# First-pass iteration of an attention backward kernel: order of the matrix products, transposes and scores on TensorE, and the e column on GpSimd

## The chip, the cores and the metric

The kernel runs on one core of a Trainium2 chip. The metric is device microseconds of one execution. Before the change the median of four runs is 932.12 us (931.36 to 933.66).

## The reference

One decode step (one query position, B = 2, H = 32 heads, 4096 cached positions, head size 128) of a block with layer norm, attention and a small MLP, and the gradients of all its inputs. What costs time is the cache: K and V have 64 pairs (b, h) of 1 MB each, and their gradients are of the same size.

```python
scores = jnp.einsum("bhqd,bhkd->bhqk", q, k) * (Dh ** -0.5)
p = _softmax(scores, axis=-1)
o = jnp.einsum("bhqk,bhkd->bhqd", p, v)
...
h = x + _A_ref(_layernorm(x, axis=-1), A_k_cache, A_v_cache, A_wq, A_wo)
h2 = h + _B_ref(_layernorm(h, axis=-1), B_w1, B_w2)
...
_out, _vjp = jax.vjp(_f, A_x, A_k_cache, A_v_cache, A_wq, A_wo, B_w1, B_w2)
```

## The kernel before, in words

**Two passes.** The first pass goes over the 64 pairs once. For a pair it reads K and V (1 MB each, laid out as 128 partitions x 32 chunks x 128), computes scores, softmax numerators, the attention output, and two things that the backward pass needs later: a 128x128 matrix m = V^T (e K) with one more column for V^T e, and u = e^T K. The second pass goes over the pairs again, reads V (`Wt`; the last 6 and 5 heads of the two batches are kept in SBUF instead), and writes the gradients gK and gV, 1 MB each. It starts while the first pass is still running: from first-pass iteration 41 (`P2_AT = H + 2 + 7`) on, every second iteration carries one second-pass pair ("mixed" stage), and after the first pass the second runs alone.

**An iteration of the first pass** (`p1_iter`, lines 463 to 587) is software-pipelined over three pairs. For the newest pair (`c`, pair i) it makes scores; for the pair before (`p`, pair i-1) it makes the exponentials e and the product e K; for the pair before that (`r`, pair i-2) it makes m and u. This document uses short names for the groups of TensorE work:

- T0 to T3: `transpose_group`, eight 128x128 transposes of K chunks into a PSUM bank (L416). Two banks take turns. Each group is then copied to SBUF (`t_sb`, called KT0 to KT3 here) by ScalarE (L421), or the fourth by VectorE (L419) while i < 33.
- S0 to S3: `matvec_group`, eight matmuls with one column that make 8 x 128 scores from KT0 to KT3 (L427).
- M0 to M7: `m_part`, four matmuls with 129 columns each (L471).
- u: `u_part`, eight matmuls (L496).
- mx: one matmul that spreads the row maxima (L513). It needs `rmax` of pair i-1, a VectorE reduction (L562) over the scores after S3.

After mx come, one after the other, `nb` (VectorE, L515), the exponential `ep` (ScalarE, L521), and two products `pk` = e K of half a pair each (`pk_half(0)` and `pk_half(1)`, VectorE, L478). Into the 129th column of each `pk` half goes e itself (the "e column", `pk_tile`, L486). A copy of e for the second pass goes to `P_bf` (L567; on GpSimd while i < 41, then on VectorE).

**What sets the order.** The schedule is manual: each engine runs its instructions in the order in which the program emits them. `p1_iter` is a generator with eight steps, k = 0 to 7. After each step the main loop (L1185 to L1202) calls `pump` (which emits the next loads on the SP queue, as far as buffers have been given back), emits background work (`bg_step`: layer norm, MLP, the L650 reductions on VectorE, called ttr here), and in the mixed stage one or two steps of the second-pass generator `p2_iter` (after steps 1, 3, 4 and 6). On TensorE the order before is

T0 T1 | mx M0 | S0 T2 M1 | S1 M2 T3 | u M3 S2 M4 | M5 S3 | M6 | M7

with a bar where a step ends. On VectorE it is nb, pk_half(0), KT3 copy (while i < 33), rmax, pk_half(1).

**Buffers.** Twelve 1 MB SBUF buffers serve K, V and W loads. A K buffer is given back after `pk_half(1)` of the next iteration (L571), a V buffer after M7 two iterations later (L581), and kept V tiles are not given back until the second pass has used them. The `pk` halves take turns in three buffers, so `pk_half(1)` and its e column must wait until M3 and u have read the half that was in that buffer.

Of the kernel before, what the change touches and what calls it, by code (L numbers as in the profile page):

```python
# [15 lines left out]
def kernel(  # L16
# [20 lines left out]
    nc = tc.nc  # L37
# [15 lines left out]
    HALF = NSC // 2  # L53
    GH = 8
    OG = 4
# [17 lines left out]
    def pst(shape, dtype, role, name):  # L73

        k = banks[role].pop(0)
        banks[role].append(k)
        return ps.tile(shape, dtype, tag=f"bank{k}", bufs=1, name=name)
# [19 lines left out]
    def goes_to(tag):  # L97

        if owned[tag] > wanted.get(tag, len(pools)):
            for other in homes:  # L100
                if owned[other] < wanted.get(other, 0):
                    return other
        return tag

    def give(t, to=None):
        tag, k, _ = home_of.pop(id(t))
        to = to or goes_to(tag)
        owned[tag] -= 1
        owned[to] += 1
        free[to] += 1  # L110
        homes[to].append(k)
        given_at[k] = step[0]
# [92 lines left out]
    rt = cols.tile([128, B, H], FP32)  # L205
# [3 lines left out]
    P_bf = cols.tile([128, B * H, NSC], BF16)  # L209
# [194 lines left out]
    def warm(dst, nat, g, busy):  # L404


        for k in range(busy):
            nc.tensor.matmul(dst, lhsT=nat[:, g * GT, :],
                             rhs=nat[:, g * GT + 4 * k:g * GT + 4 * k + 4, :].rearrange("p a b -> p (a b)"),
                             start=True, stop=True)  # L410

    def transpose_group(nat, g, dve=False, busy=0):
        t_ps = pst([128, GT, 128], BF16, "tps", "t_ps")
        warm(t_ps[:].bitcast(FP32).rearrange("p a b -> p (a b)"), nat, g, busy)
        for j in range(GT):
            nc.tensor.transpose(t_ps[:, j, :], nat[:, g * GT + j, :], ident_bf[:])  # L416
        t_sb = mats.tile([128, GT, 128], BF16, tag="XT", bufs=5, name="t_sb")
        if dve:
            nc.vector.tensor_copy(out=t_sb[:], in_=t_ps[:])  # L419
        else:  # L420
            nc.scalar.copy(out=t_sb[:], in_=t_ps[:])  # L421
        return t_sb

    def matvec_group(dst, t_sb, g, vec):
        for j in range(GT):
            sc = g * GT + j
            nc.tensor.matmul(dst[:, sc:sc + 1], lhsT=t_sb[:, j, :], rhs=vec, start=True, stop=True)  # L427
# [35 lines left out]
    def p1_iter(i, dve_group, busy):  # L463

        c = S1[i] if i < NP1 else None
        p = S1[i - 1] if 1 <= i <= NP1 else None
        r = S1[i - 2] if i >= 2 else None

        def m_part(k):
            for sc in range(4 * k, 4 * k + 4):  # L470
                nc.tensor.matmul(r["m"][:, 0:129], lhsT=r["V"][:, sc, :],  # L471
                                 rhs=r["pk"][sc // HALF][:, sc % HALF, 0:129],
                                 start=(sc == 0), stop=(sc == NSC - 1))

        def pk_half(k):

            sl = slice(k * HALF, (k + 1) * HALF)
            nc.vector.tensor_tensor(  # L478
                out=p["pk"][k][:, :, 0:128].rearrange("p s (a two) -> p s a two", two=2),
                in0=p["K"][:, sl, :].rearrange("p s (a two) -> p s a two", two=2),  # L480
                in1=p["ep"][:, sl, None, :].to_broadcast([128, HALF, 64, 2]), op=ALU.mult)

        def pk_tile(k):

            pk = pkp.tile([128, HALF, 130], BF16, tag="pK", bufs=3, name="pk")
            nc.scalar.copy(out=pk[:, :, 128:129], in_=p["ep"][:, k * HALF:(k + 1) * HALF, 0:1])  # L486
            p["pk"].append(pk)

        def u_part():

            br, hr = pairs[i - 2]
            if hr == 0:
                u_bank[0] = pst([128, 512], FP32, "u", "u_ps")
            for k in range(8):
                g = k % 4
                nc.tensor.matmul(u_bank[0][32 * g:32 * g + H, :], lhsT=hot[:, H - 1 - hr:2 * H - 1 - hr],  # L496
                                 rhs=r["pk"][k // 4][:, 4 * g:4 * g + 4, 0:128],
                                 start=(hr == 0 and k < 4), stop=(hr == H - 1 and k >= 4))

        if c is not None:  # L500
            b, h = pairs[i]
            q = qc[:, h, b:b + 1]
            c["KT0"] = transpose_group(c["K"], 0, busy=busy)
            c["KT1"] = transpose_group(c["K"], 1)
        yield
        if r is not None:
            r["m"] = pst([128, 132], FP32, "m", "m_ps")
        if p is not None:

            bp, hp = pairs[i - 1]  # L510
            bhp = bp * H + hp
            mx = p["bank"][:, 64:192]
            nc.tensor.matmul(mx, lhsT=p["rmax"][:].to_broadcast([128, 128]), rhs=neg_ident[:], start=True, stop=True)  # L513
            nb = small.tile([128, 1], FP32, tag="nb", name="nb")
            nc.vector.tensor_reduce(out=nb[:], in_=mx, axis=AX.X, op=ALU.min)  # L515
        if r is not None:
            m_part(0)
        yield
        if p is not None:
            ep = small.tile([128, NSC, 2], BF16, tag="ep", name="ep")  # L520
            nc.scalar.activation(out=ep[:], in_=p["s"][:, :, None].to_broadcast([128, NSC, 2]),  # L521
                                 func=ACT.Exp, bias=nb[:], scale=SCALE, accum_out=es[:, bp, hp:hp + 1])
            p["ep"] = ep
            p["pk"] = []
            pk_tile(0)
        if c is not None:
            c["bank"] = pst([128, 512], FP32, "sps", "s_ps")
            c["s"] = c["bank"][:, 0:NSC]
            matvec_group(c["s"], c.pop("KT0"), 0, q)
            c["KT2"] = transpose_group(c["K"], 2, busy=busy)  # L530
        if r is not None:
            m_part(1)
        yield
        if c is not None:
            matvec_group(c["s"], c.pop("KT1"), 1, q)
        if p is not None:
            pk_half(0)
        if r is not None:
            m_part(2)
        if c is not None:  # L540
            c["KT3"] = transpose_group(c["K"], 3, dve_group)
        yield
        if r is not None:
            u_part()
            m_part(3)
        if c is not None:
            matvec_group(c["s"], c.pop("KT2"), 2, q)
        if r is not None:
            m_part(4)
        if p is not None and hp % OG == OG - 1:  # L550

            totp = p["bank"][:, 256:256 + OG]
            nc.tensor.matmul(totp, lhsT=half_f32, rhs=es[:, bp, hp + 1 - OG:hp + 1], start=True, stop=True)
        yield
        if p is not None:
            pk_tile(1)
        if r is not None:
            m_part(5)
        if c is not None:
            matvec_group(c["s"], c.pop("KT3"), 3, q)  # L560
            rmax = small.tile([128, 1], BF16, tag="rmax", name="rmax")
            nc.vector.reduce_max(out=rmax[:], in_=c["s"], axis=AX.X)  # L562
            c["rmax"] = rmax
        if p is not None:
            if hp % OG == OG - 1:
                nc.vector.reciprocal(out=rt[:, bp, hp + 1 - OG:hp + 1], in_=totp)
            (nc.gpsimd if i < P2_AT else nc.vector).tensor_copy(out=P_bf[:, bhp, :], in_=ep[:, :, 0])  # L567
        yield
        if p is not None:
            pk_half(1)  # L570
            give(p["K"])  # L571
        if r is not None:
            m_part(6)
        yield
        if r is not None:
            br, hr = pairs[i - 2]
            m_part(7)
            if (br, hr) in kept:
                S2.setdefault(turn_of[(br, hr)], {})["W"] = r["V"]
            else:  # L580
                give(r["V"])  # L581
            MT = wop.tile([128, 128], BF16, tag="MT", bufs=NMT, name="MT")
            nc.scalar.copy(out=MT[:], in_=r["m"][:, 0:128])  # L583
            nc.scalar.copy(out=OU[:, br, hr:hr + 1], in_=r["m"][:, 128:129])
            MTs[(br, hr)] = MT
            del S1[i - 2]
        yield
# [471 lines left out]
    P2_AT = H + 2 + M0_ITERS  # L1059
# [4 lines left out]
    i = j = 0  # L1064
# [61 lines left out]
    for n, (i, j) in enumerate(plan):  # L1126
# [44 lines left out]
        if i is None:  # L1171
            spread[0] = 2
            at_k[0] = 1
            k = 0
# [71 lines left out]
```

## Time and profile before

| what | value |
|---|---|
| median of four runs | 932.12 us |
| profiled execution, its own time | 930.93 us |
| span of the profiled execution | 929.2 us |
| TensorE (matmul) busy | 759.5 us, 82% |
| VectorE busy | 660.6 us, 71% |
| ScalarE busy | 548.9 us, 59% |
| GpSimd busy | 144.0 us, 15% |
| HBM read and written | 212.16 MB and 149.13 MB, 389 GB/s over the span |
| first T0 of iterations 0, 34, 41, 49, 63 | 9.70, 221.60, 269.00, 339.40, 462.05 us |
| a first-pass iteration where nothing else is in it | 5.75 us |

Read it by stages. The first pass alone lies between 10 and 269 us, the mixed stage between 269 and about 475 us, the second pass alone behind that. Busy shares differ by stage, so the tables by windows of 10 us tell more than the sums. In the timeline a row gives start, length, engine, source line, operation, and in brackets the idle time before it with what ended it.

### The profile page before, as it was taken

To read this page: it belongs to the slowest core of one execution; us is meant where nothing else is said; L and a number is where in the kernel's file an instruction comes from. 1 tells how busy PE (TensorE), PEld (TensorE's weight loads), DVE (VectorE), ACT (ScalarE), POOL (GpSimd) and SP (SyncE) were. 2 spreads that over 40 slices of the span, in tenths; PEclk is the share of its full clock that TensorE was granted. 3 is DMA by queue.
4 is the path that set the end of the run, shared out by engine and by line. 5 is a ranking of instruction groups with operands and counts; after the bars stand their busy time and mean duration, and the time that the engine had idled before them with its cause. 6 is when DMAs were issued, how large, how long until landed. Compare 5 with 4: busy or idle time off the path is not lost.

```text
span 929.2 us, 26767 instructions
## 1 busy us (share of the span) xinstructions
PE 759.5 (82%) x11482; PEld 637.3 (69%) x11482; DVE 660.6 (71%) x1237; ACT 548.9 (59%) x1162; POOL 144.0 (15%) x249
## 2 busy tenths in 40 slices
PE   6999799999998889798868845866868887888892
PEld 5887687888787778787767735654757566666661
DVE  4655677766776868776878779968798544548774
ACT  4666565667776767675743534544746556557661
POOL 1222111121000101010012112111122101012211
PEclk9999999999998989997995776656655557556556
DMA  8999999997888999999999999999999999999998
GB/s 347 418 399 409 406 381 410 411 416 297 314 302 313 362 391 395 425 420 415 407 371 415 402 426 373 403 400 397 387 397 388 427 425 425 424 374 353 423 423 356
DMA packets 59478, 363.02 MB, mean 391 GB/s; under 512 B 5696, under 2 KB 15552, under 8 KB 19168
## 3 DMA queue, kind: packets, MB, share of 16 engines
q1 hardware_dynamic: 37920, 212.18, 58.0%
q0 software_dynamic: 18432, 134.23, 34.9%
q10 hardware_dynamic: 3008, 14.91, 4.0%
q8 instruction: 90, 1.47, 0.6%
q14 instruction: 28, 0.23, 0.1%
HBM read 212.16 MB, written 149.13 MB: 389 GB/s over the span
## 4 chain that ended last, share of the span: by engine, by line
PE 36%; DMA 33%; DVE 15%; ACT 9%; issue 5%; POOL 0%; SPq 0%; POOLq 0%; ACTq 0%; DVEq 0%
DMA Kt<-in_A_k_cache_dram 16%; PE t_ps L437 8%; DMA out_dram<-gK 7%; DMA out_dram<-gV 7%; PE m_ps L471 6%; PE t_ps L416 6%; ACT t_sb L421 4%; DVE gV L823 4%; DVE gK L823 3%; PE s_ps L427 3%; DMA wqs<-in_A_wq_dram 3%; PE o_ps L927 3%; DVE junk L650 2%; DVE pk L478 2%; PE u_ps L496 2%
## 5 line engine op out<-in xcount | busy, mean ns | idle before, releaser
L421 ACT COPY t_sb<-t_ps 128x1024 bf16<-128x1024 bf16 x223 | 216.6, 1012 | 45.6 <-PE t_ps L416 41.0
L442 ACT COPY t_sb<-t_ps 128x512 f32<-128x512 f32 x256 | 149.6, 587 | 147.4 <-PE t_ps L437 144.6
L437 PE MATMUL t_ps<-ident_f,Wt 128*128 128x128 f32 x848 | 193.7, 376 | 2.0 <-ACT t_sb L421 1.4
L471 PE MATMUL m_ps<-pk,Vt 128*128 128x129 bf16 x2048 | 192.0, 223 | 1.0 <-DVE pk L478 0.6
L478 DVE TENSOR_TENSOR pk<-Kt,ep 128x2048 bf16<-128x2048 bf16 x128 | 156.3, 1221 | 34.8 <-ACT ep L521 34.7
L823 DVE TENSOR_TENSOR gK<-rb,gsp 128x2048 bf16<-128x2048 bf16 x128 | 152.2, 1224 | 28.5 <-DMA out_dram<-gK 16.9
L416 PE MATMUL t_ps<-ident_bf,Kt 128*128 128x128 bf16 x2048 | 154.0, 226 | 16.5 <-DMA Kt<-in_A_k_cache_dram 16.4
L823 DVE TENSOR_TENSOR gV<-rb,pp 128x2048 bf16<-128x2048 bf16 x128 | 152.5, 1217 | 20.6 <-DMA out_dram<-gV 17.6
L437 PEld LDWEIGHTS t_ps<-ident_f,Wt 128*128 128x128 f32 x848 | 134.6, 195 | 26.6 <-issue 18.9
L471 PEld LDWEIGHTS <-Vt 128*128 128x128 bf16 x2048 | 129.0, 99 | 29.0 <-issue 29.0
L416 PEld LDWEIGHTS <-Kt 128*128 128x128 bf16 x2048 | 126.8, 101 | 19.0 <-DMA Kt<-in_A_k_cache_dram 18.7
L450 PEld LDWEIGHTS <-t_sb 128*128 128x128 bf16 x2048 | 96.1, 106 | 37.9 <-ACT t_sb L442 18.3
L427 PE MATMUL s_ps<-qc,t_sb 128*128 128x1 bf16 x2048 | 88.9, 164 | 18.9 <-ACT t_sb L421 17.3
L450 PE MATMUL dp_ps<-gom,t_sb 128*128 128x2 bf16 x2048 | 95.0, 167 | 9.3 <-ACT t_sb L442 8.3
L427 PEld LDWEIGHTS <-t_sb 128*128 128x128 bf16 x2048 | 75.2, 97 | 31.5 <-ACT t_sb L421 27.8
L880 POOL DMA_DIRECT2D out_dram<-gV x64 | 34.2, 534 | 276.8 <-DVE gV L823 229.5
L861 POOL DMA_DIRECT2D out_dram<-gK x64 | 34.0, 532 | 276.8 <-DVE gK L823 213.0
L567 POOL COPY P_bf<-ep 128x32 bf16<-128x32 bf16 x40 | 42.6, 1064 | 219.3 <-ACT ep L521 219.3
L936 ACT CAST ot<-o_ps 128x512 bf16<-128x512 f32 (+4 forms) x134 | 59.5, 479 | 15.4 <-DMA out_dram<-ot 9.6
L562 DVE TENSOR_REDUCE rmax<-s_ps 128x1 bf16<-128x32 f32 x64 | 12.3, 192 | 61.0 <-PE s_ps L427 60.9
L650 DVE CUSTOM_DVE_ANT_0 junk<-wo_t,hbc 128x640 bf16<-128x640 bf16 x64 | 52.3, 817 | 0.2
L583 ACT CAST MT<-m_ps 128x128 bf16<-128x128 f32 x64 | 17.0, 266 | 58.9 <-PE m_ps L471 58.9
(194 smaller groups left out, 815.7 us busy)
## 6 DMA issues: line engine op xcount, KB each, us to landing
Kt<-in_A_k_cache_dram SPq DMA_DIRECT2D x64, 1024.0 KB, 14.6
Vt<-in_A_v_cache_dram SPq DMA_DIRECT2D x64, 1024.0 KB, 12.9
out_dram<-gV POOLq DMA_DIRECT2D x64, 1024.0 KB, 11.9
out_dram<-gK POOLq DMA_DIRECT2D x64, 1024.0 KB, 11.0
Wt<-in_A_v_cache_dram SPq DMA_DIRECT2D x53, 1024.0 KB, 13.5
wo_t<-in_A_wo_dram SPq DMA_DIRECT2D x4, 1280.0 KB, 19.3
wqs<-in_A_wq_dram SPq DMA_DIRECT2D x5, 1024.0 KB, 19.2
wq_t<-in_A_wq_dram SPq DMA_DIRECT2D x5, 960.0 KB
```

The source lines that it names most:

```text
L416: nc.tensor.transpose(t_ps[:, j, :], nat[:, g * GT + j, :], ident_bf[:])
L421: nc.scalar.copy(out=t_sb[:], in_=t_ps[:])
L427: nc.tensor.matmul(dst[:, sc:sc + 1], lhsT=t_sb[:, j, :], rhs=vec, start=True, stop=True)
L437: nc.tensor.transpose(t_ps[:, j, :], natf[:, 2 * cc:2 * cc + 2, :].rearrange("p c k -> p (c k)"), ident_f[:])
L442: nc.scalar.copy(out=t_sb[:], in_=t_ps[:])
L450: nc.tensor.matmul(dst[:, sc:sc + 2], lhsT=v[:, j, :, par], rhs=vecs[:, par, :], start=(par == 0), stop=(par == 1))
L471: nc.tensor.matmul(r["m"][:, 0:129], lhsT=r["V"][:, sc, :], rhs=r["pk"][sc // HALF][:, sc % HALF, 0:129], start=(sc == 0), stop=(sc == NSC ...
L478: nc.vector.tensor_tensor(out=p["pk"][k][:, :, 0:128].rearrange("p s (a two) -> p s a two", two=2), in0=p["K"][:, sl, :].rearrange("p s (a ...
L567: (nc.gpsimd if i < P2_AT else nc.vector).tensor_copy(out=P_bf[:, bhp, :], in_=ep[:, :, 0])
L650: nc.vector.tensor_tensor_reduce(out=junk[0:kc, 0:width], in0=in0, in1=in1, scale=1.0, scalar=0.0, op0=ALU.mult, op1=ALU.add, accum_out=acc)
L823: nc.vector.tensor_tensor(out=pairs_view(dst[:, sl, :]), in0=row.rearrange("p (a two) -> p a two", two=2)[:, None, :, :].to_broadcast([128 ...
L936: nc.scalar.copy(out=ot[0:P, k, n0:n0 + nn], in_=o_ps[0:P, 0:nn])
```

## The change

Inside `p1_iter` the same instructions are emitted in another order, and the e column goes to another engine while i < 41. On TensorE the order after is

T0 T1 | mx M0 M1 | T2 S0 | M2 S1 T3 | u M3 S2 M4 | M5 M6 | M7 S3 | (nothing)

`pk_tile(1)`, the reciprocal, the `P_bf` copy, `pk_half(1)` and the giving back of the K buffer are now in step 5 ahead of M5; `rmax` is in step 6 after S3. So VectorE has nb, pk_half(0), KT3 copy, pk_half(1), rmax. The two e columns of a pair are copied by GpSimd while i < 41. The SP queue has the same instructions in the same order.

```diff
+            col, e = pk[:, :, 128:129], p["ep"][:, k * HALF:(k + 1) * HALF, 0:1]
+            if i < P2_AT:
+                nc.gpsimd.tensor_copy(out=col, in_=e)
+            else:
+                nc.scalar.copy(out=col, in_=e)
-            nc.scalar.copy(out=pk[:, :, 128:129], in_=p["ep"][:, k * HALF:(k + 1) * HALF, 0:1])
...
             m_part(0)
+            m_part(1)
         yield
...
         if c is not None:
+            c["KT2"] = transpose_group(c["K"], 2, busy=busy)
             c["bank"] = pst([128, 512], FP32, "sps", "s_ps")
             c["s"] = c["bank"][:, 0:NSC]
             matvec_group(c["s"], c.pop("KT0"), 0, q)
-            c["KT2"] = transpose_group(c["K"], 2, busy=busy)
+        yield
         if r is not None:
-            m_part(1)
-        yield
+            m_part(2)
+        if p is not None:
+            pk_half(0)
         if c is not None:
             matvec_group(c["s"], c.pop("KT1"), 1, q)
-        if p is not None:
-            pk_half(0)
-        if r is not None:
-            m_part(2)
-        if c is not None:
             c["KT3"] = transpose_group(c["K"], 3, dve_group)
         yield
...
         if p is not None:
             pk_tile(1)
+            if hp % OG == OG - 1:
+                nc.vector.reciprocal(out=rt[:, bp, hp + 1 - OG:hp + 1], in_=totp)
+            (nc.gpsimd if i < P2_AT else nc.vector).tensor_copy(out=P_bf[:, bhp, :], in_=ep[:, :, 0])
+            pk_half(1)
+            give(p["K"])
         if r is not None:
             m_part(5)
+            m_part(6)
+        yield
+        if r is not None:
+            m_part(7)
         if c is not None:
             matvec_group(c["s"], c.pop("KT3"), 3, q)
             rmax = small.tile([128, 1], BF16, tag="rmax", name="rmax")
             nc.vector.reduce_max(out=rmax[:], in_=c["s"], axis=AX.X)
             c["rmax"] = rmax
-        if p is not None:
-            if hp % OG == OG - 1:
-                nc.vector.reciprocal(out=rt[:, bp, hp + 1 - OG:hp + 1], in_=totp)
-            (nc.gpsimd if i < P2_AT else nc.vector).tensor_copy(out=P_bf[:, bhp, :], in_=ep[:, :, 0])
-        yield
-        if p is not None:
-            pk_half(1)
-            give(p["K"])
-        if r is not None:
-            m_part(6)
         yield
         if r is not None:
             br, hr = pairs[i - 2]
-            m_part(7)
```

## The prediction

> **What bounds the kernel now.** I read the page first (span, rows by slice, chain), then the SP queue's issues, then windows of 10 us, then the timeline of single iterations.
>
> ```profile
> span 929.2 us, 26767 instructions
> ...
> DMA  8999999997888999999999999999999999999998
> GB/s 347 418 399 409 406 381 410 411 416 297 314 302 313 362 391 395 425 420 415 407 371 415 402 426 373 403 400 397 387 397 388 427 425 425 424 374 353 423 423 356
> ...
> PE 36%; DMA 33%; DVE 15%; ACT 9%; issue 5%; POOL 0%; SPq 0%; POOLq 0%; ACTq 0%; DVEq 0%
> ```
>
> A slice is 23.2 us. The DMA engines are full nearly everywhere; only in slices 10 to 14 (209 to 325 us) do they fall to 297 to 362 GB/s. Time can be won there, or where the loads catch up with the work. The windows show what is full instead (columns: PE, PEld, DVE, ACT, POOL busy, clock, DMA share, GB/s):
>
> ```profile
> 210.00:220.00 10.00, 9.27 (x177) 7.85 (x176) 5.88 (x9) 7.67 (x18) 2.41 (x2) 1.00 0.99 392
> 220.00:230.00 10.00, 9.62 (x192) 8.65 (x188) 7.01 (x26) 7.21 (x15) 0.33 (x2) 1.00 0.55 208
> 250.00:260.00 10.00, 9.13 (x170) 7.29 (x168) 9.79 (x29) 8.55 (x18) 0.77 (x2) 1.00 0.84 306
> 300.00:310.00 10.00, 9.14 (x162) 8.34 (x161) 9.86 (x23) 7.83 (x18) 1.71 (x2) 0.87 0.95 359
> 360.00:370.00 10.00, 9.15 (x190) 8.29 (x188) 7.10 (x12) 7.46 (x18) 0.53 (x1) 1.00 1.01 421
> ```
>
> So: DMA until 220 us, TensorE at 220 to 240, VectorE around 250 and 300, DMA again from about 325. Now an iteration with nothing else in it (timeline):
>
> ```profile
> 26.28 0.94 PEld L416 LDWEIGHTS <-Kt 128*128 128x128 bf16 x16
> 26.98 1.93 ACT L421 COPY t_sb<-t_ps 128x1024 bf16<-128x1024 bf16 x2
> 27.23 0.22 PE L513 MATMUL s_ps<-neg_ident,rmax 128*128 128x128 bf16 x1
> 28.04 0.27 PEld L427 LDWEIGHTS <-t_sb 128*128 128x128 bf16 x8 [0.54 <-ACT t_sb L421]
> ...
> 31.79 0.19 DVE L562 TENSOR_REDUCE rmax<-s_ps 128x1 bf16<-128x32 f32 x1 [0.72 <-PE s_ps L427]
> 31.90 1.21 DVE L478 TENSOR_TENSOR pk<-Kt,ep 128x2048 bf16<-128x2048 bf16 x1
> 32.02 0.94 PEld L416 LDWEIGHTS <-Kt 128*128 128x128 bf16 x16
> ```
>
> TensorE has one hole, 0.54 us, in which S0 waits for the copy of T0. VectorE idles 0.72 us for S3 and only then starts pk_half(1). The last two views are the chain around 250 us and the mixed stage's VectorE:
>
> ```profile
> 249.33 1.14 DVE pk L478
> 250.47 0.02 issue
> 250.48 5.01 DMA Kt<-in_A_k_cache_dram
> ```
>
> ```profile
> 310.38 1.22 DVE L478 TENSOR_TENSOR pk<-Kt,ep 128x2048 bf16<-128x2048 bf16 x1
> 314.28 0.19 DVE L562 TENSOR_REDUCE rmax<-s_ps 128x1 bf16<-128x32 f32 x1 [2.68 <-PE s_ps L427]
> 314.38 0.17 DVE L567 COPY P_bf<-ep 128x32 bf16<-128x32 bf16 x1
> 314.47 1.22 DVE L478 TENSOR_TENSOR pk<-Kt,ep 128x2048 bf16<-128x2048 bf16 x1
> ```
>
> From 217 us on the end of pk_half(1) gives back the K buffer that the next K load waits for: pk_half(1) ends at 250.47, the load is issued at 250.48, lands 5.01 us later, and T0 of iteration 39 starts at once. In an iteration with second-pass work VectorE stands idle for 2.68 us with pk_half(1) queued behind rmax.
>
> **The change, part by part.**
>
> *TensorE, one plain iteration.* Steps from start to start in the iteration above (T0 at 0): T0 T1 mx 0.95; S0 starts at 1.76, when KT0 is there; S0 0.20, T2 0.41, M1 0.31, S1 0.19, M2 0.20, T3 0.60, u 0.55, M3 0.19, S2 0.23, M4 M5 0.44, S3 0.23, M6 M7 0.43: together 5.74. After: M0 M1 run to 0.95 + 0.47 = 1.42, T2 then needs T0's bank, which the same copy frees, so it starts at 1.76. Then T2 2.17, S0 2.37, M2 2.67 (taken at M1's price behind S0), S1 2.86, T3 3.46, u 4.01, M3 4.20, S2 4.43, M4 to M6 5.09, M7 5.30, S3 5.53. The hole shrinks from about 0.54 to 0.34, as M1 now lies in it: 0.2 us an iteration. KT1 (ready at 2.63) is in time for S1 at 2.67, KT2 (4.07, and 0.11 earlier without the column on ScalarE) for S2 at 4.20.
>
> *rmax behind pk_half(1).* The change makes mx of the next iteration wait for more. pk_half(1) needs VectorE (KT3 copy ends at 31.07, that is 4.79) and M3 with u (4.42): it runs 4.8 to 6.0, rmax ends at 6.1 to 6.2. mx loads its weights 0.89 into the next iteration, at 5.53 + 0.89 = 6.42. Margin 0.2 to 0.3 us; another 0.34 us of lateness falls into the hole ahead of T2. Queued behind rmax on VectorE are ttr, nb and then pk_half(0); nb stands behind the same instructions in both orders. The ttr of 0.82 + 0.08 us covers the way rmax, mx, nb; where there is none, ep is held anyway by ScalarE's two copies (until 2.63).
>
> *e column on GpSimd.* 80 ScalarE copies of 262 ns go (21 us of ScalarE, which the page's chain does not list). On GpSimd the nearest row is the P_bf copy: 40 copies, 209 ns alone, 1266 ns beside a pk. The new queue there is column, column, P_bf per iteration, at most 3 x 1.27 = 3.8 us of a 5.5 us iteration. The second column waits for M3 and u, and P_bf is behind it; nobody needs either before the next iteration's M4 or the second pass. GpSimd's stores (gK, gV) start at 282 us, after the last column at about 267 us, so no store waits behind one. Where a 209 ns copy got in just ahead of a pk (120.07 and 170.65 us), that pk took 1.25 instead of 1.22: 80 x 0.03 = 2.4 us of VectorE time in all; I take 0, as VectorE has 0.72 us free per plain iteration.
>
> The Trainium skill, SBUF — State Buffer, section "SBUF: two separate sides", speaks against this part: VectorE with two SBUF inputs and GpSimd share a port pair under an exclusive lock, and whichever starts second fully blocks. The 1266 ns beside a pk agree with GpSimd as the blocked one; the pk of 1.25 us behind a 209 ns copy shows hardly any block the other way. By the rule VectorE could lose up to 80 x 0.2 = 16 us as an estimate, and a few us of it in the VectorE-bound stretches, so the gain would nearly vanish; by the rows it stays.
>
> *K given back earlier.* In a plain iteration pk_half(1) ends at 6.0 instead of 31.90 + 1.21 = 6.8; in a mixed one it fills the idle 2.68. SP's order is unchanged, so V loads behind K move with it.
>
> *The sum by stages.* (1) Until T0 of iteration 34 (221.60): DMA-bound. That iteration's K, issued at 204.97, landed at 219.85 by its mark (the page's median of 14.6 us gives 219.6), with the DMA full, so no order of work can start T0 sooner: gain between 0 and 1.75, the plain saving 13 x 0.2 = 2.6 since the last wait at 143 us exceeds it: 1.7. (2) Iterations 34 to 40: 0.2 each in the five that TensorE or the load sets (34, 35, 36, 39, 40), 0 in 37 and 38, where VectorE runs without gaps (9.79 of 10): 1.0. Ends: -0.2 x 7 if mx is late (see the first rival), +0.8 x 7 if each K came as much earlier as its buffer. (3) Iterations 41 to 48, four pairs of iterations. With second-pass work, the second pass's second group of transposes waits for ScalarE in either order (0.58 us at 273.99); gain only through VectorE, where pk_half(1) leaves the queue ahead of gV: 314.47 + 1.22 = 315.69 becomes about 314.8, of which I keep 0.3; the plain one gains 0.2. 4 x 0.5 = 2.0; ends 0 and 4 x 1.22 = 4.9. (4) From iteration 49 (339.40) on DMA is full at 421 GB/s: 0, with up to +1 at 440 to 480 us, where windows fall to 368 and 305 GB/s. The second pass alone has unchanged instructions and starts earlier by the sum. Sum: 1.7 + 1.0 + 2.0 = 4.7 us. The profiled execution took 930.93 us, so 926.2; it lies 1.2 under the median of 932.12, which makes **927.4 us**.
>
> **The rivals.**
>
> *rmax holds mx (slower).* Where VectorE is late, rmax comes a whole pk (1.22 us) later than today, and mx stands in front of all of TensorE's queue. In iteration 38 rmax would move from 249.22 to 250.44 against a mx due at 249.99; with M0 and M1 (0.47) T2 starts at 251.1 instead of 250.86: 0.2 lost. It decides from the point where rmax ends 0.6 us after mx's turn. For it: five ttr an iteration in stage 2, two gV or gK halves in stage 3. Against it: VectorE's total is unchanged, and 32.1 us of it were idle before rmax in the mixed stage. Price: 0.18 x 32 iterations from 34 on, 5.8, less 1.7 of stage 1: about 936.
>
> *The loads hide it (no change).* If stages 3 and 4 are bound by DMA earlier than I think (share 0.95 to 1.00 at 300 to 330 already), only 1 or 2 us come through: 931.
>
> *The K buffer is worth more.* From 220 to 320 us the windows fall 11 MB short of 420 GB/s, which is 27 us of full rate. If the earlier K release recovers a third: 923.
>
> **How the numbers follow.** Forecast 0.45, rmax rival 0.25, loads hide it 0.2, larger gain 0.1. A measurement tells about 0.2% from no change, that is 1.9 us. Faster is forecast and larger gain, 0.55; same 0.2; slower 0.25. The likeliest case alone spans 924.5 to 930 (stages 2 and 3 at 0.5 and 1.5 of their values, stage 1 at 0 or 1.7). The range for all reaches to 936 on the slow side and a little past 923 on the fast side: 922 to 936.
>
> **What would show it.** The wait of S0 for the copy goes and a smaller one, about 0.3 us, stands before T2; plain iterations of 5.5 us among the first ones (T0 to T0); rmax no longer waits on S3 for 2.7 us in mixed iterations; K issues follow pk_half(1) 0.8 to 1.8 us earlier; T0 of iteration 34 at about 220, of 41 at 266, of 49 at 334 to 335. Wrong it would be if mx waits on rmax by more than 0.3 us in most iterations, if pk grows beyond 1.25 us, or if T0 of 41 is early and T0 of 63 is not.

## The result, and the profile after

The changed kernel takes 925.75 us (median of 44 runs, 920.87 to 933.12), the kernel before 931.36 us (63 runs, 926.4 to 938.7). The ratio is 0.9945, with a 95% interval of 0.9931 to 0.9959: 5.1 us less, between 3.8 and 6.4. The profiled execution of the changed kernel took 925.08 us, with a span of 923.3 us against 929.2.

The page after: span, DMA by slice of 23.1 us, and the shares of the chain that ended last.

```profile
span 923.3 us, 26951 instructions
...
DMA  8999999998789999999999999999999999999998
GB/s 346 417 400 411 404 393 410 412 414 322 305 305 364 357 399 423 422 421 422 415 382 394 369 426 398 402 385 405 390 372 383 427 424 425 424 391 370 421 419 358
...
PE 36%; DMA 31%; DVE 15%; ACT 10%; issue 6%; POOL 1%; ACTq 0%; POOLq 0%; DVEq 0%; SPq 0%
```

The share of DMA in the chain falls from 33% to 31%, and the slices from 208 to 416 us carry more bytes than before in six places of nine. The windows say it more sharply (columns: PE, PEld, DVE, ACT, POOL busy, clock, DMA share, GB/s):

```profile
220.00:230.00 10.00, 9.81 (x208) 9.24 (x206) 8.48 (x32) 7.09 (x13) 4.05 (x6) 1.00 0.66 234
250.00:260.00 10.00, 9.34 (x185) 7.91 (x185) 9.74 (x27) 7.12 (x14) 2.67 (x6) 1.00 0.92 346
300.00:310.00 10.00, 8.41 (x134) 7.71 (x135) 8.25 (x16) 7.72 (x15) 2.24 (x3) 0.83 0.84 315
```

Before, 208 and 306 GB/s were moved at 220 and 250 us; now 234 and 346. A window at the same time no longer holds the same work at 300 us (the work there is over 4 us further on), so from there on iterations are compared, not windows. A plain iteration, in the timeline of the changed kernel:

```profile
26.25 0.90 PEld L416 LDWEIGHTS <-Kt 128*128 128x128 bf16 x16
...
27.98 0.43 PEld L416 LDWEIGHTS <-Kt 128*128 128x128 bf16 x7 [0.25 <-issue]
28.37 0.30 PEld L427 LDWEIGHTS <-t_sb 128*128 128x128 bf16 x8
...
30.98 1.21 DVE L478 TENSOR_TENSOR pk<-Kt,ep 128x2048 bf16<-128x2048 bf16 x1
...
31.77 0.51 PEld L416 LDWEIGHTS <-Kt 128*128 128x128 bf16 x9
...
32.12 0.18 DVE L573 TENSOR_REDUCE rmax<-s_ps 128x1 bf16<-128x32 f32 x1
```

S0 (28.37) starts without a wait, the hole of 0.25 us now stands before T2 (27.98), pk_half(1) starts at 30.98 instead of 31.90, rmax ends behind it, and the iteration is 5.52 us long instead of 5.74. Over the whole run, the waits of TensorE's weight loads for KT copies at L427 fall from 27.8 us in 54 places to 3.2 us in 2, as the lists of waits of the kernel before and of the changed one show:

```profile
PEld L427 <- ACT t_sb L421: 27.8, 54, 0.7
```

```profile
PEld L427 <- ACT t_sb L421: 3.2, 2, 2.7
```

The waits of VectorE between 266 and 475 us (columns: engine, line and what it waited for; us in total, times, longest), before:

```profile
DVE rmax L562 <- PE s_ps L427: 32.1, 13, 4.6
DVE nb L515 <- PE s_ps L513: 7.7, 5, 3.3
DVE gK L823 <- DMA out_dram<-gV: 5.7, 1, 5.7
```

and after:

```profile
DVE pk L478 <- PE m_ps L471: 11.5, 11, 2.0
DVE nb L519 <- PE s_ps L517: 10.8, 6, 4.5
DVE rmax L573 <- PE s_ps L427: 5.7, 11, 0.7
...
DVE gV L823 <- DMA out_dram<-gK: 2.9, 1, 2.9
DVE gK L823 <- DMA out_dram<-gV: 2.0, 1, 2.0
```

26 us of waiting for S3 are gone from rmax. 11.5 us of them come back as a wait of pk_half(1) itself, which now reaches the head of the queue before M3 and u have read its buffer, and 3 us as a wait of nb. The fourth kind is one single stall: gK waits for the store of gV, 5.7 us before and 2.0 after.

| first T0 of iteration | before, us | after, us | earlier by |
|---|---|---|---|
| 34 | 221.60 | 221.26 | 0.3 |
| 41 | 269.00 | 267.88 | 1.1 |
| 43 | 283.97 | 282.74 | 1.2 |
| 44 | 298.28 | 293.58 | 4.7 |
| 49 | 339.40 | 334.26 | 5.1 |
| 63 | 462.05 | 455.84 | 6.2 |

Of the 5.9 us by which the span is shorter, 3.5 appear in iteration 43 alone (14.31 us long before, 10.84 after). There the first second-pass pair stores its gradients, and it is the only place between 266 and 475 us where gK waits for gV's store (a second one, at 486 us, lies behind the first pass: 4.1 us before, 1.5 after). The chain of waits there, before:

```profile
280.65 1.22 DVE gV L823
281.87 0.30 issue
282.17 10.36 DMA out_dram<-gV
292.53 0.03 issue
...
292.62 0.22 DVE gK L823
```

and after:

```profile
279.33 1.22 DVE gV L823
280.55 0.30 issue
280.85 6.63 DMA out_dram<-gV
287.49 0.03 issue
...
287.58 0.22 DVE gK L823
```

At that time the stores own one buffer, so gK can be written only when gV has left it. gV is stored 1.32 us earlier than before, but the store of the same 1 MB is over 5.04 us earlier. Why that store takes 10.4 us in the one kernel and 6.6 in the other became the main question.

### The profile page after: what moved, and what is told of

It is laid out like the page before. It is cut to its first block, busy times and chain, and to the rows that moved or that the text cites. A ratio compares the mean times of both kernels' runs of the same rounds, so it can differ in the third digit from the quotient of the medians.

```text
span 923.3 us, 26951 instructions
## 1 busy us (share of the span) xinstructions
PE 756.0 (82%) x11482; PEld 635.9 (69%) x11482; DVE 662.4 (72%) x1237; ACT 530.0 (57%) x1082; POOL 167.1 (18%) x329
## 4 chain that ended last, share of the span: by engine, by line
PE 36%; DMA 31%; DVE 15%; ACT 10%; issue 6%; POOL 1%; ACTq 0%; POOLq 0%; DVEq 0%; SPq 0%
DMA Kt<-in_A_k_cache_dram 17%; DMA out_dram<-gK 10%; PE t_ps L437 9%; PE t_ps L416 6%; PE m_ps L471 6%; DVE gV L823 4%; DVE gK L823 4%; DMA out_dram<-gV 4%; ACT t_sb L421 4%; PE o_ps L927 3%; ACT t_sb L442 2%; PE s_ps L427 2%; DVE junk L650 2%; PE dp_ps L450 2%; DVE pk L478 2%
## 5 line engine op out<-in xcount | busy, mean ns | idle before, releaser
L478 DVE TENSOR_TENSOR pk<-Kt,ep 128x2048 bf16<-128x2048 bf16 x128 | 156.3, 1221 | 54.2 <-ACT ep L526 26.7
L471 PE MATMUL m_ps<-pk,Vt 128*128 128x129 bf16 x2048 | 172.5, 223 | 1.3 <-ACT OU L584 1.1
L471 PEld LDWEIGHTS <-Vt 128*128 128x128 bf16 x2048 | 126.6, 99 | 29.7 <-issue 29.7
L488 POOL COPY pk<-ep 128x16 bf16<-128x16 bf16 x80 | 61.5, 770 | 196.6 <-ACT ep L526 162.6
L427 PE MATMUL s_ps<-qc,t_sb 128*128 128x1 bf16 x2048 | 88.0, 164 | 4.9 <-ACT t_sb L421 2.9
L427 PEld LDWEIGHTS <-t_sb 128*128 128x128 bf16 x2048 | 77.4, 97 | 7.7 <-ACT t_sb L421 3.2
L850 ACT ACTIVATE rb<-dp_ps,rt 128x256 bf16<-128x256 f32 x64 | 30.4, 475 | 36.6 <-PE dp_ps L845 35.9
```

Source lines behind the costliest of these rows:

```text
L471: nc.tensor.matmul(r["m"][:, 0:129], lhsT=r["V"][:, sc, :], rhs=r["pk"][sc // HALF][:, sc % HALF, 0:129], start=(sc == 0), stop=(sc == NSC ...
L478: nc.vector.tensor_tensor(out=p["pk"][k][:, :, 0:128].rearrange("p s (a two) -> p s a two", two=2), in0=p["K"][:, sl, :].rearrange("p s (a ...
L488: nc.gpsimd.tensor_copy(out=col, in_=e)
```

## The experiments

All kernels below keep the work and differ in order alone, except where an engine or a wait is named. Names of parts: FRONT is M1 ahead of T2, T2 ahead of S0, M2 ahead of S1; EARLY is pk_half(1), with the P_bf copy and the giving back of K, ahead of M5, S3 and rmax; TAIL is S3 behind M6 and M7; POOLCOL is the e column on GpSimd. The change is all four. Differences in us are the ratio's distance from 1 times 931.

**Which part is it? EARLY alone, FRONT alone, and the change without EARLY.**

```diff
# early_only
         if p is not None:
             pk_tile(1)
+            rest_of_e()      # reciprocal, P_bf
+            pk_half(1)
+            give(p["K"])
         if r is not None:
             m_part(5)
         if c is not None:
             rmax_of()        # S3, rmax
...
-        if p is not None:
-            pk_half(1)
-            give(p["K"])
         if r is not None:
             m_part(6)
# front_only: M1 after M0; T2 ahead of S0; M2 ahead of S1
# no_early: the change, with pk_half(1) and give behind rmax again
```

> Order of before on TensorE, column on ScalarE; only the VectorE part is done: reciprocal, P_bf, pk_half(1) and the giving back of K stand in step 5 ahead of M5, S3 and rmax. VectorE-queue theory (the gain is pk_half(1) no longer standing behind rmax; the stores and K loads of the mixed stage start earlier): 3 to 5 us under before, T0 of iteration 49 at 334.5 to 336.5 us, idle before rmax in the mixed stage well under 32 us. TensorE-hole theory (the gain is the shorter wait ahead of S0): within 1.5 us of before, T0 of 49 at 338 to 340.

> Only the front of the TensorE order is changed (M1 ahead of T2, T2 ahead of S0, M2 ahead of S1); S3, rmax, pk_half(1) and the column on ScalarE as before. TensorE-hole theory: plain iterations of 5.5 us and 3 to 5 us under before. VectorE-queue theory: plain iterations of 5.5 us as well, but no more than 1.5 us under before, since DMA holds the first 220 us and VectorE most of the rest.

> The changed kernel, with rmax put back ahead of pk_half(1) on VectorE (TensorE order and GpSimd column stay as changed, so S3 is last and pk_half(1) now starts only after it). VectorE-queue theory: the gain is lost, and as S3 is later than before, pk_half(1) and the K release come 0.3 to 0.5 us later than before in each iteration: -1 to +4 us against before. TensorE-hole theory: 2 to 4 us under before remain, since TensorE's order is the changed one. rmax-holds-mx rival: this is faster than the changed kernel, since mx no longer waits for a pk.

| kernel | median, us | before on the same chip | ratio and interval |
|---|---|---|---|
| early_only | 925.24 | 931.35 | 0.9935 [0.9910, 0.9959] |
| front_only | 929.34 | 931.35 | 0.9976 [0.9960, 0.9991] |
| no_early | 932.22 | 931.35 | 1.0012 [0.9992, 1.0032] |

EARLY alone gives 6.1 us, as much as the whole change and more than the 3 to 5 I had expected. T0 of iteration 49 stands at 337.35 us in its profile, which misses my 334.5 to 336.5; that profile is of the slowest of its 12 runs and was 1.1 us behind before at T0 of iteration 34. FRONT alone gives 2.2 us (expected: no more than 1.5; the interval is 0.8 to 3.7), and its plain iterations are 5.5 us long, so the hole of TensorE was real but little of it reaches the end. Everything but EARLY gives nothing: 1.1 us slower, with an interval that holds 0. EARLY's 6.1 and that -1.1 make the 5.1 of the whole within the intervals; no_early contains FRONT, so FRONT's 2.2 do not come on top of EARLY there.

**Where is it? The changed order in the mixed stage alone, and in the first pass alone.**

```diff
# mixed_part: the changed order (no GpSimd column) only where i >= P2_AT
# first_part: the change, column included, only where i < P2_AT
```

> The changed order only from iteration 41 on (the mixed stage); the first 41 iterations as before, no column on GpSimd anywhere. By my prediction's sum 2.0 us under before. By the profile after (1.1 us gained up to T0 of iteration 41, 5.1 up to T0 of 49) 3.5 to 5 us under before, with T0 of 41 at 269 us and T0 of 49 at 335 to 336.

> The whole change, GpSimd column included, but only in iterations below 41 (order of before from 41 on). The prediction gave these stages 1.7 + 1.0 = 2.7 us; the profile of after shows T0 of iteration 41 only 1.1 us earlier than before. Theory (the first 34 iterations are held by the loads, so only the last seven count): T0 of iteration 41 0.8 to 1.3 us earlier, iteration 43 still 14 us or more, kernel 0.5 to 1.5 us under before. Rival (the first pass is worth what the prediction said): 2.7 us under.

mixed_part took 926.34 us, ratio 0.9944 [0.9920, 0.9969]: a gain as large as the whole one is there without one changed iteration before 41. first_part took 928.89 us (before: 930.11), ratio 0.9983 [0.9959, 1.0007]: 1.6 us with an interval that holds 0 as well as the predicted 2.7. In its profile T0 of iteration 41 stands at 269.26 us, no earlier than before's 269.00, which misses my 0.8 to 1.3; iteration 43 took 13.40 us and gK waited 5.4 us for gV's store.

**Is it the one stall? EARLY in iteration 41 alone, and everywhere but there.** The pk_half(1) of iteration 41 gives back the K buffer that the last load pair before gV's store waits for.

```diff
# early_41:     EARLY only where i == 41
# early_not_41: EARLY everywhere but i == 41
```

> Order of before everywhere, but in iteration 41 alone pk_half(1) and the giving back of K stand ahead of M5, S3 and rmax. One-stall theory (most of the gain is iteration 43, where gK waits for the store of gV in the only buffer that the stores own by then, and that store lands sooner because the K load of iteration 43 is issued sooner): iteration 43 lasts 10.8 to 11.5 us instead of 14.3, 3 to 4 us under before. Many-iterations theory (each mixed iteration gains some 0.3 us from VectorE's idle time): iteration 43 gains at most 1 us, 0 to 1 us under before.

> The opposite: pk_half(1) early in all iterations but 41. One-stall theory: iteration 43 at about 14 us again, 1 to 3 us under before. Many-iterations theory: 5 to 6 us under before, as with all iterations.

early_41 took 929.07 us (before 930.77), ratio 0.9969 [0.9948, 0.9991]: moving one pk_half(1) in one of the 64 pairs is worth 2.9 us. early_not_41 took 929.31 us, ratio 0.9985 [0.9960, 1.0010]. The chain of waits at the store, first early_41, then early_not_41:

```profile
281.63 6.86 DMA out_dram<-gV
```

```profile
282.77 10.65 DMA out_dram<-gV
```

In early_not_41 rmax's wait in the mixed stage is down to 5.9 us in total, as in the changed kernel, and yet iteration 43 takes 15.38 us; in early_41 rmax still waits 29.5 us, and iteration 43 takes 10.88. So iteration 43's length goes with that one move and not with rmax's waits in the other iterations. The two ratios together make 4.3 us of early_only's 6.1, within what their intervals allow; about half of the gain is that stall. Where the other half comes from is not shown: early_not_41's interval holds 0.

**Take the stall away by other means: a second buffer for the stores.**

```diff
# g_buffer_before: order of before
-            give(p["K"])
+            give(p["K"], "g" if i == 41 else None)
```

> Order of before, but the K buffer that iteration 41 gives back goes to the stores instead of the loads, so that gK of the first second-pass pair need not wait for the store of gV. One-stall theory: the wait of VectorE's gK for the store (5.7 us) goes, iteration 43 shortens by 3 to 5 us, unless the load that misses the buffer (K of iteration 43, which then waits for a V buffer) takes its place; 2 to 5 us under before. Many-iterations theory: within 1.5 us of before.

934.41 us, ratio 1.0037 [1.0015, 1.0058]: 3.4 us slower, where I had expected 2 to 5 us less. The stall is gone (gK no longer waits for a store, iteration 43 takes 10.89 us), but the loads lack the buffer: V of iteration 42 is issued at 286.65 us instead of 279.10, and soon the first pass waits for K, which this line of its chain shows:

```profile
296.62 8.86 DMA Kt<-in_A_k_cache_dram
```

So the stall can't be bought off with this load buffer.

**Why is the store 10 us in one order and 7 in the other? The next load pair held back.** In before, the loads of K44 and V43 are issued 3.3 us behind the store, and I took the store's last packets to stand behind them.

```diff
# hold_load: order of before
+            if i == 43:      # ScalarE reads K44's buffer once more, after ep
+                nc.scalar.copy(out=hold_sb[:], in_=held[0][:, 0, 0:1])
...
-            pump()
+            if not (i == 42 and k >= 6 or i == 43 and k < 2):
+                pump()
```

> Order of before, all work the same, but the two loads that iteration 43 issues for K and V of iteration 44 are held back by some 3.5 us: the buffer of K is kept by a one-column ScalarE copy behind the exponentials of iteration 43, and the loads are asked for later. In before they are issued at 285.4 and 285.9 us, while the last 70 KB or so of the gV store (issued 282.2) are still to be written. Theory (the store's tail stands behind the next pair of loads): store issue to gK start 5.5 to 7 us instead of 10.4, iteration 43 about 11 us instead of 14.3, kernel 2 to 4 us under before, though the later K44 may give some of it back in iteration 44. Rival (the store takes its 10 us whatever the loads do, and after's earlier pk_half(1) shortens iteration 43 in another way): store to gK 10 us or more, iteration 43 14 us or more, kernel 0 to 3 us over before.

934.58 us (before 930.11), ratio 1.0028 [1.0004, 1.0052]. The SP queue and the chain of hold_load:

```profile
282.11 0.33 SPq L460 DMA_DIRECT2D Kt<-in_A_k_cache_dram  x1
282.53 0.38 SPq L460 DMA_DIRECT2D Vt<-in_A_v_cache_dram  x1
292.24 0.33 SPq L460 DMA_DIRECT2D Kt<-in_A_k_cache_dram  x1
```

```profile
285.60 9.58 DMA out_dram<-gV
295.23 0.04 issue
295.28 0.22 DVE gK L868
```

The next pair was issued 6.6 us behind the store instead of 3.3, and no packet of it moved before 7.5 us; the store still took 9.58 us. (The expectation also had the store wrongly as all but written when that pair is issued in before: by the packets, 1 of its 128 had ended 3.3 us behind the issue.) My theory of the next pair falls: it could be 0.8 us of the 3.7. The rival as I had put it did not hold to the letter either (9.67 us to gK and an iteration of 13.2 us, where it said 10 and 14 or more), but it was right that the next loads do not set the store's time.

What remains is the pair ahead. The traces list every DMA packet, and for each kernel I worked out from them how long before gV's store K43 was issued, how many 8 KB packets of that load pair (256) began later than 1 us after the store's issue, and when the store's last packet ended:

| kernel | K43 ahead of the store, us | load packets begun over 1 us behind the store's issue | store's last packet, us after its issue |
|---|---|---|---|
| before, no_early, front_only, early_not_41, first_part, pool_only, hold_load | 3.50 in each | 105 to 110 | 9.1 to 9.9 |
| early_only, early_41, early_front, early_front_pool | 4.56 to 4.63 | 63 to 84 | 6.4 to 7.4 |
| changed kernel, mixed_part | 4.82, 4.89 | 38, 40 | 6.2, 6.0 |
| g_buffer_before (V42 not ahead of the store: issued 3.3 us behind it) | 4.00 | none of K43's 128 | 5.6 |

The sorting has no exception in fourteen kernels. Where pk_half(1) of iteration 41 is ahead of rmax, K43 has a lead of 4.6 to 4.9 us and 15 to 33% of the pair's packets begin over 1 us behind the store's issue; where it is behind, the lead is 3.50 us and two fifths of the pair are still to come then. In the second row it is K43's lead that differs; V42 is issued 3.26 us ahead of the store there and 3.08 in the first row. In before, the first packet of the store moves 2.9 us after its issue, against 1.7 in the changed kernel. That the store follows the pair ahead is a reading of these packets, made from runs that were meant to tell other things apart; it was not tested by a run of its own.

One rival can be settled by the kept traces: that VectorE's order behind the store's issue sets the store's time. early_front and early_not_41 have the same order there. Their VectorE rows behind the issue (at 281.48 and 282.77 us) stand at the same distance from it, first early_front, then early_not_41:

```profile
281.83 1.25 DVE L483 TENSOR_TENSOR pk<-Kt,ep 128x2048 bf16<-128x2048 bf16 x1
283.13 1.21 DVE L483 TENSOR_TENSOR pk<-Kt,ep 128x2048 bf16<-128x2048 bf16 x1
```

```profile
283.12 1.25 DVE L483 TENSOR_TENSOR pk<-Kt,ep 128x2048 bf16<-128x2048 bf16 x1
284.41 1.21 DVE L483 TENSOR_TENSOR pk<-Kt,ep 128x2048 bf16<-128x2048 bf16 x1
```

Yet the store's last packet ends 6.5 us behind the issue in the one and 9.9 in the other, and K43's lead is 4.63 against 3.50. early_41, with rmax ahead of the second product there as in before, has 6.4.

**The other parts by themselves: the e column on GpSimd, and S3.**

```diff
# pool_only:        order of before, POOLCOL
# early_front:      FRONT and EARLY, S3 ahead of M6 and M7 as before, column on ScalarE
# early_front_pool: the same with POOLCOL, that is the change without TAIL
```

> Order of before, the e column alone on GpSimd in iterations below 41. Theory (ScalarE was not the bound and VectorE is hardly blocked by GpSimd's small copies): within 1.5 us of before, pk mean 1.22 us as in before. Rival (GpSimd blocks VectorE for the 0.2 us of each of 80 copies): pk mean 1.25 or more and 1 to 3 us over before. If ScalarE's 21 us did count: 1.5 to 3 us under.

> pk_half(1) early and the changed front of the TensorE order, but S3 back ahead of M6 and M7 and the column on ScalarE. If the parts add up: 6 to 8 us under before (6.1 from the early pk_half(1), 2.2 from the front), 1 to 2 us under the changed kernel, since rmax then comes sooner. If they fall on the same waits: 5 to 6 us under before.

> The changed kernel with one part undone: S3 stands again ahead of M6 and M7, as in before; pk_half(1) stays ahead of rmax, the products ahead of T2 and S0, the column on GpSimd. Theory (moving S3 last is worth nothing by itself, since rmax is behind pk_half(1) anyhow): 5 to 7 us under before, within 2 us of the changed kernel (5.2 under). Rival (S3 last is what lets pk_half(1) go first without mx being late): 2 us or more slower than the changed kernel, so 3 us or less under before.

| kernel | median, us | before on the same chip | ratio and interval |
|---|---|---|---|
| pool_only | 931.53 | 930.11 | 1.0014 [0.9992, 1.0036] |
| early_front | 924.78 | 930.77 | 0.9928 [0.9906, 0.9951] |
| early_front_pool | 925.99 | 930.11 | 0.9930 [0.9906, 0.9954] |

The column on GpSimd can't be told from no change. Its cost groups in pool_only (busy us, mean ns, idle before):

```profile
L483 DVE TENSOR_TENSOR pk<-Kt,ep 128x2048 bf16<-128x2048 bf16 x128 | 156.2, 1221 | 35.6 <-ACT ep L545 23.1 <-issue 10.5 <-POOL pk L493 1.9
```

```profile
L493 POOL COPY pk<-ep 128x16 bf16<-128x16 bf16 x80 | 57.7, 724 | 204.3 <-ACT ep L545 180.4 <-PE m_ps L476 22.0 <-DVE pk L483 1.4
```

pk takes 1221 ns, as in before (156.3 us in 128), so VectorE lost nothing; GpSimd's copies stretch to 724 ns on average, and nobody waits for them but 1.9 us of pk. Without TAIL the kernel is as fast as the change or a little faster: 6.7 and 6.5 us under before, against 5.1, which the intervals don't separate. S3 last is not needed.

## Why the prediction was right or wrong

The predicted 927.4 us, from a sum of 4.7 us, stands beside 925.75 and 5.1. That closeness is luck: stage 1 gave 1.4 us less than its term, stage 3 gave 2.0 us more, and most of stage 3's came from a stall that no term of the sum held.

**Plain iteration: right.** 5.53 predicted, 5.52 seen, hole 0.34 predicted and 0.25 seen, before T2 as said.

**Stage 1: wrong.** "The plain saving 13 x 0.2 = 2.6 since the last wait at 143 us exceeds it: 1.7." It was 0.3 in the profile. K of iteration 34 landed when predicted, 219.94 us against 219.85 before. But the step counted 13 iterations of saving since 143 us, as if no K bound in between. In the trace of before none does: T0 of iteration 32 starts at 209.95 us without a wait. With the shorter iterations its K is late, though, as the timeline of the changed kernel shows:

```profile
210.04 0.73 PE L416 MATMUL t_ps<-ident_bf,Kt 128*128 128x128 bf16 x10 [1.10 <-DMA Kt<-in_A_k_cache_dram]
```

T0 starts 0.1 us later than before, and what had been saved is gone; two iterations are left to gain in. That K had no margin to give: by the traces' landing marks it landed at 209.91 us in before, 0.04 ahead of its T0, and at 210.00 in the changed kernel. Nor was the saving whole up to there. At iteration 21 the changed kernel stood 0.3 us behind before, and in iteration 27 it lost 0.8 us to a wait for which the profile names no cause:

```profile
185.73 0.10 PEld L427 LDWEIGHTS <-t_sb 128*128 128x128 bf16 x1 [0.98 <-issue]
```

I bounded the stage by the landing of one K, that of iteration 34, and asked of no K ahead of it how much margin it had. front_only and no_early, with plain iterations of 5.5 us, have T0 of iteration 34 at 221.44 and 221.42; they stood over 2 us behind before at iteration 22, and T0 of iteration 32 waits for K in no_early (0.39 us) and not in front_only.

**Stage 2: right in size.** 1.0 predicted, 0.8 in the profile (T0 34 to 41: 47.4 us before, 46.6 after). One profile of each would not carry that: first_part, with the same order there, shows 47.4. But the six profiles with FRONT in these iterations show 46.6 to 47.4, with a median of 46.9, and the eight without it 47.4 to 48.3, with a median of 47.6. early_only and early_not_41, which release K earlier there but have no FRONT, show 47.7, so the gain comes with FRONT.

**Stage 3: half of what came, and for another reason.** 2.0 predicted, 4.0 seen (T0 41 to 49: 70.4 to 66.4 us). 3.5 of the 4.0 are iteration 43. The other seven iterations took 55.5 us instead of 56.1, where the sum had 1.7 for them; over all kernels but g_buffer_before, of either order, they take 54.1 to 58.5, so no gain there is shown. In iteration 41 the term was put rightly: pk_half(1) leaves the queue ahead of gV, and gV starts 1.33 us earlier at 277.24, of which 1.12 was there at T0 of that iteration. What failed is the end of that step. I took an earlier gV for a saving of 0.3 us each time, and asked of the stores only whether they wait behind a column on GpSimd. I did not ask who waits for the store. gK does, for the stores' one buffer, and the row of 5.7 us stood in VectorE's list of waits before, third from the top. Nor did I ask what an earlier K load does there: "K given back earlier" was costed only for T0. In iteration 41 it put the load pair 1.3 us further ahead of gV's store, and the store was over 3.7 us sooner after its issue; that the one caused the other is the reading of the packets above. The mechanism is nearest to the rival "the K buffer is worth more"; its 9 us of spread-out full-rate transfer didn't come, its one place did.

**Stage 4: nearly right.** 0 predicted; 1.1 us more were gained between T0 of iterations 49 and 63, and nothing behind 63. That stretch takes 120.5 to 123.6 us over the fourteen profiles, so I don't explain it.

**GpSimd's column: right.** Costed at 0; measured 1.3 us slower with an interval that holds 0. The Trainium skill, SBUF — State Buffer, section "SBUF: two separate sides", would have made VectorE pay up to 16 us by my estimate; pk stayed at 1221 ns with 80 more copies of GpSimd beside it, and in the changed kernel 26 of the products start while a GpSimd copy is running and still take 1220 ns on average. So here the measurement decides: GpSimd is the one that is held up (724 and 770 ns a copy on average, against 253 to 258 where VectorE runs nothing beside it), VectorE isn't.

**The rival "rmax holds mx": fell.** Weight loads of mx waited for rmax 2.9 us in all from 217 us on, at most 0.7 each, where I had priced 0.18 x 32 = 5.8; 0.9 us of it lies in the mixed stage. In iterations 34 to 40 it is 2.0 us in three places, so the mechanism exists where VectorE runs without gaps, as its condition said; but no_early, which puts rmax ahead of pk_half(1) again, is some 6 us slower than the changed kernel, not faster. **"The loads hide it"** fell too: mixed_part, changed in the mixed stage alone, has a gain as large as the whole one. T0 of iteration 41 came at 267.88 instead of 266, which is stage 1's miss; T0 of 49 came at 334.26, as said.

## What to carry to other kernels

An instruction that waits at the head of an in-order queue costs what stands ready behind it. Here moving 1.2 us of ready work in front of a wait was worth as much as the whole rearrangement, while a hole closed on TensorE in every iteration was worth 2 us; in front_only's profile 0.2 us of what it saved in the first 34 iterations was left at T0 of iteration 34. When a step gives a buffer back earlier, follow the transfer that it releases as far as the next store or load behind it, and ask for each store who waits until it is done. The longest single waits in the list are worth such a question even when they occur once.

## What the hardware showed that was not expected

A 1 MB store issued while a load pair is still moving takes far longer than its bytes. Store packets of 8 KB take 309 ns at the median (314 in g_buffer_before), which for 128 of them on 16 engines is 2.5 us; yet the last one ended 9.6 us after the issue in before. Three things can be seen in the packets. The store starts as the loads ahead of it run out. The load packets begun more than 1 us behind the store's issue take 374 to 428 ns on average in the seven kernels with the short lead, though 309 to 327 at the median; those of the pair begun earlier take 359 to 394 on average, so it is not the store alone that makes them slow. And the DMA engines then seem to get out of step: in hold_load, with no load packet under way between 5.5 and 7.5 us after the issue, the packets of the store in flight fall from 12 to 6, 6 and 2, and one at a time goes on until 9.1 us. So the time of such a store looks to be that of the engine that comes last. The Trainium skill, DMA: Bandwidth & Descriptors, section "Why a DMA increments its semaphore by 16 and not by 1", says that up to 16 engines run a transfer and finish independently, and that the waiting side needs them all; that agrees with gK in hold_load starting 9.67 us after the issue, 0.6 behind the last packet. Why some load packets slow down, and why the engines drift apart, stays open.
